# A transformer block on one core: transposes moved from TensorE to DMA, LN2 scale and shift in place, weight loads by rows

## The chip, the cores and the metric

The kernel runs on 1 core of one Trainium2 chip. The metric is device time in microseconds (us), the median of several runs. A profile is one execution; its span (first to last instruction) is about 1.8 us shorter than the device time. Engines: PE is TensorE (PEld its weight loads), DVE is VectorE, ACT is ScalarE, POOL is GpSimd, SP issues most DMAs. ACTq and SPq are the DMA-issuing instructions on ACT and SP. A packet is one record of a DMA engine; a transfer "lands" when its last packet has told its semaphore. Tile names in the profile's lines: soft holds the attention weights, pa is their product with v, xn a normalised token tile, hT the transposed LN2 rows, pacc the sums of wo or fc1.

## The reference

One diffusion-transformer block in bf16, B=2 batches of N=256 tokens, D=1152, two heads, F=4608:

```
mod = silu(c) @ w_mod                       # shift/scale/gate for attention and for the MLP
h   = layernorm(x) * (1 + scale_a) + shift_a
q, k, v = h @ wqkv
a   = softmax(q k^T / sqrt(576)) v @ wo
x   = x + gate_a * a
h2  = layernorm(x) * (1 + scale_m) + shift_m       # "LN2"
out = x + gate_m * (gelu(h2 @ w_fc1) @ w_fc2)
```

The 512 tokens are 4 token tiles of 128 (tiles 0, 1 are batch 0; tiles 2, 3 are batch 1). A matmul contracts over partitions, so two results have to be transposed: the attention weights before they meet v, and the normalised LN2 rows before they meet w_fc1.

## The kernel before

Weights stream from HBM through five buffers of 2.65 MB, all issued by SP in order: a buffer is loaded again as soon as its last reader is done. A section is loaded by rows (2304 contiguous bytes each) or by column panels (768 bytes each):

```python
    def load_section(name, s):                       # rows: 3 x 1152 elements
        for r in range(0, KD, 3):
            nc.sync.dma_start(w[:, r:r + 3, :], wmod_v[:, r:r + 3, s * D:(s + 1) * D])
    def load_panels(name, view, col0):               # panels: 9 x 384 elements
        for n in range(NPD):
            nc.sync.dma_start(w[:, :, n * PW:(n + 1) * PW], view[:, :, col0 + n * PW:col0 + (n + 1) * PW])
    ...
    w_v = load_panels("w_v", wqkv_v, 2 * D)
    w_o = load_panels("w_o", wo_v, 0)
    w_f1[0] = load_panels("w_f1_0", wfc1_v, 0)       # ... and w_f1[1]
    # ... after the v matmuls: w_f1[2], w_f1[3], w_gate_m
```

Attention weights are transposed on TensorE (16 matmuls against an identity) and evicted from PSUM. LN2 is transposed the same way, in pieces placed between the matmuls of wo (batch 0) and of the first fc1 outputs (batch 1); the eviction applies scale and shift:

```python
    def ln2_transpose(b, ks, eng):
        pt = aux_tile([P, len(ks), N], "pt", BF16)               # 2 PSUM buffers of this kind
        for i, k in enumerate(ks):
            for tl in range(TPB):
                nc.tensor.transpose(pt[:, i, tl * P:(tl + 1) * P], xn2[b * TPB + tl][:, k * P:(k + 1) * P], ident[:])
        for i, k in enumerate(ks):       # ACT or DVE: hT = pt * scale_m + shift_m
            ...
    order = [(t, i) for t in range(NT) for i in range(NPD)]      # 12 wo groups: token tile, column panel
    for o, (t, i) in enumerate(order):
        wo_group(t, i, ...)              # 9 matmuls; DVE: tmp = acc * gate; POOL: x1 = tmp + x
        if o: ln2_stats(*order[o - 1])   # DVE statistics; after a tile's last panel: sqrt (ACT), normalise
    ...
    MSPLIT = 10                          # first 10 fc1 outputs batch by batch, the others on 512 tokens
```

## Time and profile before

| | before |
|---|---|
| device time, median (3 runs) | 250.02 us (249.83 to 250.53) |
| span of the profile | 248.3 us |
| PE busy | 239.7 us |
| wo matmuls | 82.2 to 101.0 us |
| first fc1 matmul | 100.8 us |
| largest PE gap after the start | 0.99 us |

Lines of the page of the kernel before: the span, PE's busy time, and the chain of work that ended last, by engine.

```profile
span 248.3 us, 4032 instructions
PE 239.7 (97%) x1734; PEld 144.9 (58%) x1745; DVE 63.9 (26%) x172; ACT 69.1 (28%) x135; POOL 30.8 (12%) x46
PE 91%; DMA 3%; ACT 2%; DVE 1%; issue 1%; SPq 0%; ACTq 0%; DVEq 0%
```

PE bounds the kernel. The windows view of the kernel before shows the LN2 hand-over (columns: stretch, its length, busy us of each engine with the number of instructions, granted clock, DMA share of the 16 engines, GB/s):

```profile
100.00:108.00 8.00, 8.00 (x78) 6.98 (x76) 4.69 (x15) 5.15 (x8) 0.74 (x1) 1.00 1.10 332
108.00:116.00 8.00, 7.01 (x70) 6.19 (x68) 1.01 (x3) 5.06 (x10) 0.00 (x0) 1.00 0.80 297
```

PE is full from 100 to 108 us, has one gap of 1 us after it, and the DMA engines are full (share 1.10) beside it. The timeline of the same kernel (start, duration, engine, line, operation; in brackets the idle time before it and what ended it) names the gap:

```profile
106.04 1.28 ACT L674 ACT_TABLE_LOAD   x1
109.38 0.38 PE L582 MATMUL pt<-ident,xn 128*128 128x128 bf16 x4 [0.99 <-ACT hT L587]
```

PE waits for ACT to evict a transpose, and ACT is late because of a table load.

### The profile page before, as it was taken

How to read it: one execution, taken by the hardware profiler on the slowest of the kernel's cores; microseconds unless marked ns; L12 is line 12 of the kernel's file. 1: busy time of each engine (PE TensorE's matmuls, PEld its weight loads, DVE VectorE, ACT ScalarE, POOL GpSimd, SP SyncE). 2: the span in 40 equal slices, each digit the busy share in tenths (PEclk: the TensorE clock that was granted, in tenths of full speed). 3: DMA queues.
4: the chain of work that ended last, by engine and by line, in shares of the span. 5: the costliest groups of instructions: out<-in, count | busy, mean ns of one | idle time of the engine just before them, and what ended most of it. 6: DMA issues, size and time to landing. Idle time of an engine off the chain costs nothing.

```text
span 248.3 us, 4032 instructions
## 1 busy us (share of the span) xinstructions
PE 239.7 (97%) x1734; PEld 144.9 (58%) x1745; DVE 63.9 (26%) x172; ACT 69.1 (28%) x135; POOL 30.8 (12%) x46
## 2 busy tenths in 40 slices
PE   6799999999999999989999999999999999999994
PEld 2585444456657656878744444444565666656674
DVE  2852551335535588720001000000001100000001
ACT  7641341252424325593224222332000000000000
POOL 4000000021000255100003010000011122211111
PEclk9999999999999999999999999999999999999999
DMA  6999999999999999993194997490000000000000
GB/s 231 326 337 364 365 334 386 331 370 394 372 327 328 326 329 326 326 372 148 33 338 109 338 340 227 141 288 1 0 16 18 16 16 18 17 16 20 26 22 17
DMA packets 54285, 51.59 MB, mean 208 GB/s; under 512 B 1515, under 2 KB 47995, under 8 KB 54267
## 3 DMA queue, kind: packets, MB, share of 16 engines
q1 hardware_dynamic: 53664, 50.14, 64.0%
q0 software_dynamic: 576, 1.19, 1.4%
q8 instruction: 13, 0.21, 0.4%
q14 instruction: 5, 0.04, 0.1%
q10 hardware_dynamic: 27, 0.00, 0.0%
HBM read 50.14 MB, written 1.19 MB: 207 GB/s over the span
## 4 chain that ended last, share of the span: by engine, by line
PE 91%; DMA 3%; ACT 2%; DVE 1%; issue 1%; SPq 0%; ACTq 0%; DVEq 0%
PE pacc L704 28%; PE pacc L658 25%; PE pacc L488 7%; PE pacc L611 7%; PE pacc L436 7%; PE pk L265 5%; DMA w_scale_a<-in_w_mod_dram 3%; PE pk L298 2%; PE pa L544 2%; PE ps_s L464 2%; PE pn L381 1%; PE pg L414 1%; PE pm L233 1%; PE pt L243 1%; PE pt L582 1%
## 5 line engine op out<-in xcount | busy, mean ns | idle before, releaser
L704 PEld LDWEIGHTS <-gT 128*128 128x128 bf16 x468 | 44.4, 98 | 26.2
L710 DVE TENSOR_TENSOR tmp<-pacc,gate 128x384 f32<-128x384 f32 (+2 forms) x13 | 6.9, 527 | 103.8 <-PE pacc L704 103.8
L682 ACT ACTIVATE gT<-pacc 128x512 bf16<-128x512 f32 x26 | 15.5, 597 | 34.9 <-PE pacc L658 34.9
L712 POOL TENSOR_TENSOR o_sb<-tmp,x_1139 128x384 bf16<-128x384 f32 (+1 forms) x12 | 11.7, 972 | 88.9 <-DVE tmp L710 88.9
L488 PE MATMUL pacc<-w_v,hT 128*128 128x384 bf16 x108 | 19.2, 326 | 0.0
L704 PE MATMUL pacc<-w_f_2_1852,gT 128*128 128x384 bf16 (+2 forms) x117 | 18.9, 314 | 0.0
L658 PE MATMUL pacc<-hT,w_f_0_128 128*128 128x256 bf16 x162 | 18.8, 273 | 0.0
L704 PE MATMUL pacc<-w_f_1_1750,gT 128*128 128x384 bf16 x108 | 18.7, 326 | 0.0
L611 PE MATMUL pacc<-w_o,big_136 128*128 128x384 bf16 x108 | 18.5, 326 | 0.0
L704 PE MATMUL pacc<-w_f_3_1954,gT 128*128 128x384 bf16 (+2 forms) x135 | 18.4, 294 | 0.0
L704 PE MATMUL pacc<-w_f_0_1622,gT 128*128 128x384 bf16 x108 | 18.2, 326 | 0.0
L658 PE MATMUL pacc<-hT,w_f_1_132 128*128 128x512 bf16 (+1 forms) x88 | 17.9, 357 | 0.1
L436 PE MATMUL pacc<-hT,w_q 128*128 128x512 bf16 x79 | 17.7, 379 | 0.1
L658 PE MATMUL pacc<-hT,w_f_3_1047 128*128 128x512 bf16 x80 | 17.6, 379 | 0.1
L658 PE MATMUL pacc<-hT,w_f_2_1043 128*128 128x512 bf16 x79 | 17.5, 379 | 0.1
L658 PEld LDWEIGHTS <-w_f_0_128 128*128 128x128 bf16 x162 | 15.7, 98 | 1.8
L425 POOL DMA_DIRECT2D gates_dram<-nat x8 | 4.3, 543 | 79.6 <-DVE nat L422 79.6
L618 POOL TENSOR_TENSOR x_1139<-tmp,x_sb 128x384 f32<-128x384 f32 x11 | 10.0, 912 | 33.1 <-issue 27.0
L488 PEld LDWEIGHTS <-hT 128*128 128x128 bf16 x108 | 10.4, 98 | 6.3 <-issue 0.5
L611 PEld LDWEIGHTS <-big_136 128*128 128x128 bf16 x108 | 10.4, 98 | 6.2
L265 PE MATMUL pk<-big_136,w_k 128*128 128x256 bf16 (+2 forms) x88 | 13.3, 292 | 0.5 <-ACT big_136 L252 0.4
L658 PEld LDWEIGHTS <-w_f_1_132 128*128 128x128 bf16 x90 | 8.7, 98 | 8.5 <-issue 0.3
(119 smaller groups left out, 220.2 us busy)
## 6 DMA issues: line engine op xcount, KB each, us to landing
w_shift_a<-in_w_mod_dram SPq DMA_DIRECT2D x3, 864.0 KB, 11.1
w_q<-in_wqkv_dram SPq DMA_DIRECT2D x3, 864.0 KB, 12.3
w_gate_a<-in_w_mod_dram SPq DMA_DIRECT2D x3, 864.0 KB, 10.0
w_v<-in_wqkv_dram SPq DMA_DIRECT2D x3, 864.0 KB, 12.4
w_shift_m<-in_w_mod_dram SPq DMA_DIRECT2D x3, 864.0 KB, 10.2
w_scale_m<-in_w_mod_dram SPq DMA_DIRECT2D x3, 864.0 KB, 14.8
w_o<-in_wo_dram SPq DMA_DIRECT2D x3, 864.0 KB, 16.4
w_f_0_128<-in_w_fc_dram SPq DMA_DIRECT2D x3, 864.0 KB, 10.3
```

The costliest lines, as they stand in the source:

```text
L265: nc.tensor.matmul(pk[m][:, c0:c1], w_k[:, k, m * P:(m + 1) * P], hT0[:, k, c0:c1], start=(k == 0 and c0 == 0), stop=(k == KD - 1), skip_g ...
L298: nc.tensor.matmul(pk[m][:], w_k[:, k, m * P:(m + 1) * P], hT0[:, k, :], start=(k == 0), stop=(k == KD - 1),)
L436: nc.tensor.matmul(pacc[:], w_q[:, k, m * P:(m + 1) * P], hT[:, k, :], start=(k == 0), stop=(k == KD - 1),)
L464: nc.tensor.matmul(ps_s[:], qT[:, cc, q0:q0 + P], k_ap, start=(i == 0), stop=(i == len(chunks) - 1),)
L488: nc.tensor.matmul(pacc[:], hT[:, k, t * P:(t + 1) * P], w_v[:, k, pnl * PW:(pnl + 1) * PW], start=(k == 0), stop=(k == KD - 1),)
L611: nc.tensor.matmul(pacc[:], aT[:, k, t * P:(t + 1) * P], w_o[:, k, c0:c1], start=(k == 0), stop=(k == KD - 1),)
L618: (nc.gpsimd if pool_add else nc.vector).tensor_tensor(x1[:, t, c0:c1], tmp[:], x_sb[:, t, c0:c1], op=ALU.add)
L658: nc.tensor.matmul(dst, w_f1[m // KD][:, k, ml * P:(ml + 1) * P], hT[:, k, c0:c1], start=(k == 0), stop=(k == KD - 1),)
L682: nc.scalar.activation(gT[:, m, :], pacc[:], ACT.Gelu_apprx_tanh)
L704: nc.tensor.matmul(pacc[:], gT[:, kk, t * P:(t + 1) * P], w_f2[j][:, r, c0 - n * PW:c0 - n * PW + cw], start=(kk == 0), stop=(kk == KF - 1),)
L710: nc.vector.tensor_tensor(tmp[:], pacc[:], gate_m[:, b, c0:c0 + cw], op=ALU.mult)
L712: (nc.vector if last else nc.gpsimd).tensor_tensor(o_sb[:], tmp[:], x1[:, t, c0:c0 + cw], op=ALU.add)
```

## The change

The intent: take all transposes but LN1's off TensorE. Eight DMA transposes from SBUF to SBUF, issued by ACT, replace them; scale and shift are then applied in place on DVE. So that fc1 can begin while slices of hT still arrive, half of its first outputs step over the contraction (k outermost, six outputs at a time). w_v, w_o and fc1 are loaded by rows.

```diff
-    w_v = load_panels("w_v", wqkv_v, 2 * D)
+    w_v = load_rows("w_v", wqkv_v, 2 * D)          # w_o and w_f1[0..3] likewise
 ...
+    def attn_transpose(i):
+        pair = attn_all[:, TPB * i:TPB * (i + 1), :].rearrange("p i n -> p (i n)")
+        nc.scalar.dma_start_transpose(attnT_all[:, i, :].rearrange("p (c n) -> p c n", n=P), pair)
 ...                                                 # in the loop of the v groups:
+        if i >= 2 and i % 2 == 0 and i // 2 <= B * H:
+            attn_transpose(i // 2 - 1)
 ...                                                 # (16 nc.tensor.transpose and their evictions removed)
+    def ln2_modulate(b, k):
+        h = hT[:, k, b * N:(b + 1) * N]
+        nc.vector.tensor_scalar(
+            h, h, scale_m[:, k, b:b + 1], shift_m[:, k, b:b + 1], op0=ALU.mult, op1=ALU.add)
 ...                                                 # end of ln2_normalize (36 PE transposes removed):
+        nc.scalar.dma_start_transpose(hT[:, :, t * P:(t + 1) * P], xn2[:])
 ...
+    BETWEEN = {2: (0, 1), 3: (5,)}                   # scale/shift of batch 0 amid the statistics of tiles 2, 3
 ...
-    MSPLIT = 10
+    MSPLIT = 12
+    nc.scalar.activation(early_gelu[:], zeros[:, 0:1], ACT.Gelu_apprx_tanh)
+    # per batch: outputs 0..5 with k outermost, then 6..11 with k innermost;
+    # after batch 0: ln2_modulate(1, k) for all k
```

## The prediction

> **What bounds the kernel.** TensorE. The profile's first part has PE busy 239.7 of 248.3 us; the chain of waits is 91% PE. The windows by stage show granted clock 1.00 and from 84 us on one PE gap, 0.99 us, near 108.4: transposes wait for a PSUM buffer that ScalarE frees late (a gelu table load of 1.28 us at 106.0 delays it). DMA is saturated until about 112 us, but binds PE only in the first 9 us.
>
> **Removed from PE** (timeline and chain):
> - 16 transposes of the attention weights, 0.89 us.
> - 36 LN2 transposes; four take 0.22 us, so 1.98 us: half between the wo matmuls, half between the first fc1 matmuls.
> - The 0.99 us gap: nothing in fc1 waits for PSUM transposes any more, and an early gelu loads the table.
>
> Sum 3.86 us, all on the PE chain. The evictions that go too were off it.
>
> **Added or moved.** 18 in-place scale/shift operations on VectorE; the like one, hT<-big 128x256 bf16, takes 0.28 us. MSPLIT 12: two outputs as 2x256 columns instead of 512, neutral (0.109 against 0.219 us apiece in the chain). Eight DMA transposes on the ScalarE queue, 4 of 128 KB and 4 of 288 KB. No trace here times one. The Trainium skill ("DMA: Bandwidth & Descriptors", Latency and other measured facts) gives 261 GB/s with a non-contiguous middle dimension; from that I estimate 0.5 and 1.1 us of transfer, and beside saturated queues 2.5 to 5 us from issue to landing.
> Row-wise loads: a window with row sections (52 to 60 us) moves 389 GB/s, with panels (68 to 108 us) 327, so w_v, w_o and fc1 should each load about 1.2 us faster. That pays for the transposes' traffic and for needing all rows in the first group (last w_v panel landed near 53.4 us, needed by 53.8; w_o near 81.8, needed by 82.4). Stall under 0.3 us.
>
> **The critical place: LN2 into fc1.** wo should run from 81.4 to 99.0 us (12 groups of 1.465 us). Token tile 1's normalisation should end near 94.6, its transpose land at 98 to 99. VectorE waits for it in order, amid tile 2's statistics (near 97.4), and still owes two tmp, an add, three statistics, a normalise and seven modulations, about 6 us at 0.5 per large operation. fc1 eats one k slice per 0.65 us (6 matmuls of 0.109) and catches up with VectorE from k=2 to k=6. Estimated PE stall 0.5 to 2 us, about 1.1. Batch 1's transpose (issued near 104) has until 111: no stall. The attention transposes have over 6 us of slack.
>
> **Prediction.** 250.0 - 3.9 + 1.1 (hand-over) + 0.1 (loads), about 247.2 us; 8 in 10 between 245.7 and 249.4. Faster by over 2%: 0.05; within 2%: 0.91; slower by over 2%: 0.04.
>
> **What would show each step.** No PE transposes after 26 us; wo from 81.4 to 99.0; the waits list PE fc1 for VectorE hT, about 1 us, and VectorE hT for a DMA transpose, 0.5 to 2 us; PE waits for w_v or w_o under 0.3 us; PE busy near 237; DMA transposes landing in 2.5 to 5 us; GB/s near 380 between 68 and 100 us.
>
> **What would make it wrong.** A transpose that lands 8 us or later after issue (starved beside the weight stream): VectorE blocks, 250 us or more. Transposes that hold up the weight stream so that w_o lands late. Or a landing before 97: 246.1 us.

## The result

| | before | after |
|---|---|---|
| device time, median (4 runs each) | 250.11 us | 262.33 us (262.20 to 262.63) |
| ratio, 95% interval | | 1.0489 (1.0471 to 1.0507) |
| span of the profile | 248.3 us | 260.7 us |
| wo matmuls | 82.2 to 101.0 us | 82.3 to 100.1 us |
| first fc1 matmul | 100.8 us | 112.8 us |

A ratio here and below is the mean time of one kernel's runs over that of the other's of the same rounds, so not quite the ratio of the medians quoted. The outcome is slower by 4.9%, to which the prediction gave a chance of 0.04.

The page of the changed kernel, the lines that answer to those of before (and the granted clock in 40 slices of 6.5 us):

```profile
span 260.7 us, 3981 instructions
PE 239.1 (92%) x1700; PEld 144.7 (55%) x1711; DVE 66.9 (26%) x184; ACT 62.4 (24%) x124; POOL 28.0 (11%) x43
PEclk9999999999999998559999999999999999999999
PE 76%; DMA 15%; DVE 6%; ACT 1%; issue 1%; SPq 0%; DVEq 0%; ACTq 0%
```

15% of the chain is now DMA. Its windows over the same place:

```profile
92.00:100.00 8.00, 8.00 (x50) 4.63 (x48) 6.54 (x16) 1.21 (x2) 2.73 (x3) 1.00 1.09 359
100.00:108.00 8.00, 0.06 (x1) 0.00 (x0) 0.00 (x0) 0.29 (x1) 0.00 (x0) 0.66 1.08 389
108.00:116.00 8.00, 3.17 (x16) 2.28 (x17) 3.49 (x10) 1.35 (x1) 0.91 (x1) 0.50 0.70 251
```

PE, DVE and ACT stand still together from 100 to 112 us, while the DMA engines are full. The granted clock falls to half in the gap. The waits view (engine, line, what it waited for: us in all, times, longest) gives the sequence:

```profile
DVE hT L553 <- DMA hT<-xn: 16.5, 2, 13.4
PE pacc L631 <- DVE hT L553: 13.3, 2, 12.8
PE pa L541 <- DMA soft<-soft: 0.9, 1, 0.9
```

DVE waits 13.4 us for a DMA transpose, PE 12.8 us for DVE. The timeline of the changed kernel names the transpose, token tile 1's:

```profile
95.98 6.09 ACTq L573 DMA_TRANSPOSE hT<-xn  x1
112.44 0.60 DVE L553 TENSOR_SCALAR hT<-hT,scale_m,shift_m 128x256 bf16<-128x256 bf16 x2 [13.39 <-DMA hT<-xn]
112.83 5.90 PE L631 MATMUL pacc<-hT,w_f_0_128 128*128 128x256 bf16 x36 [12.78 <-DVE hT L553]
```

It was issued at 95.98 us and landed 16.4 us later. The same trace has a comparison within itself. Lines of the DMA view for 96 to 112 us, when tile 0's and tile 1's transposes move beside the weights (q1 is SP's queue, q10 ACT's: packets, MB, share of the 16 engines' time; then the issue in that window with its time to landing):

```profile
q1 hardware_dynamic: 2425, 5.36, 90.3%
q10 hardware_dynamic: 2363, 0.59, 18.6%
...
hT<-xn ACTq DMA_TRANSPOSE x1, 16.4
```

and for 116 to 117.6 us, when tile 2's moves alone; its issue, at 114.83 us, is the last line:

```profile
q10 hardware_dynamic: 1184, 0.30, 98.3%
...
hT<-xn ACTq DMA_TRANSPOSE x1, 3.2
```

Beside the stream, 2363 transpose packets of about 250 bytes (0.59 MB / 2363) went through in the time of 2425 weight packets of about 2210 bytes: one to one. It is so within the window too: from 98.4 to 103.6 us, 832 and 832. Two LN2 transposes took 16 us, 37 GB/s. Alone, one takes 1.6 us, 0.30 MB at about 185 GB/s, and lands 3.2 us after issue. The 5.36 MB that went in front are fc1 part 2's rest, part 3 and gate_m, weights that PE needed no earlier than 132 us (gate_m) and 139 us (fc1 part 2) in the kernel before.

Where the 12.4 us of span come from, each term read from the two traces:

| term | us |
|---|---|
| 52 PE transposes and the 0.99 us gap gone | -3.86 |
| PE waits for the last attention transpose | +0.88 |
| PE waits for tile 1's LN2 transpose | +12.78 |
| first 36 fc1 matmuls: 6.38 us (112.83 to 119.21) instead of 3.92 (36 x 0.109, the chain before has 8 in 0.87) | +2.46 |
| sum | +12.26 |

The last term holds both the half clock and DVE's remaining work; they are not separated here, but e2_hold below needs 6.17 us for the same matmuls at full clock, so the half clock's part seems small. The Trainium skill ("TensorE: Matmul & The Clock Gate", Part 1) says that an idle window of about 3.4 us halves the clock and about 3.4 us of work restores it. The trace agrees on the half clock and on the recovery, not on the idle time: the windows have clock 1.00 until 102.5 us, 0.50 from 102.6 to 116.2, and 1.00 after; PE had stopped at 100.1 (2.5 us before the drop, sooner than a whole window of 3.4) and begun again at 112.8 (3.4 us before the recovery).

### The profile page after: what moved, and what is told of

Its sections match the earlier page's. It is cut to its first block, busy times and chain, and to the rows that moved or that the text cites. A ratio compares the mean times of both kernels' runs of the same rounds, so it can differ in the third digit from the quotient of the medians.

```text
span 260.7 us, 3981 instructions
## 1 busy us (share of the span) xinstructions
PE 239.1 (92%) x1700; PEld 144.7 (55%) x1711; DVE 66.9 (26%) x184; ACT 62.4 (24%) x124; POOL 28.0 (11%) x43
## 4 chain that ended last, share of the span: by engine, by line
PE 76%; DMA 15%; DVE 6%; ACT 1%; issue 1%; SPq 0%; DVEq 0%; ACTq 0%
PE pacc L685 27%; PE pacc L631 25%; PE pacc L436 7%; DMA hT<-xn 6%; DMA w_f_1_132<-in_w_fc_dram 6%; PE pacc L488 6%; PE pk L265 4%; DMA w_scale_a<-in_w_mod_dram 3%; PE pk L298 2%; PE ps_s L464 2%; DVE tmp L587 1%; PE pn L381 1%; PE pg L414 1%; DVE hT L553 1%; PE pm L233 1%
## 5 line engine op out<-in xcount | busy, mean ns | idle before, releaser
L631 PE MATMUL pacc<-hT,w_f_0_128 128*128 128x256 bf16 x162 | 20.0, 287 | 13.3 <-DVE hT L553 13.3
L631 PEld LDWEIGHTS <-w_f_0_128 128*128 128x128 bf16 x162 | 16.6, 103 | 16.6 <-issue 13.9
L663 ACT ACTIVATE gT<-pacc 128x512 bf16<-128x512 f32 x24 | 14.3, 597 | 32.2 <-PE pacc L631 32.2
L631 PE MATMUL pacc<-hT,w_f_1_132 128*128 128x256 bf16 (+1 forms) x106 | 17.9, 325 | 0.1
L436 PE MATMUL pacc<-hT,w_q 128*128 128x512 bf16 x79 | 17.7, 379 | 0.1
L582 PE MATMUL pacc<-w_o,big_136 128*128 128x384 bf16 x108 | 17.7, 326 | 0.0
L582 PEld LDWEIGHTS <-big_136 128*128 128x128 bf16 x108 | 10.6, 98 | 6.9
L631 PEld LDWEIGHTS <-w_f_1_132 128*128 128x128 bf16 x108 | 10.5, 98 | 6.8 <-issue 0.3
L488 PEld LDWEIGHTS <-hT 128*128 128x128 bf16 x108 | 10.4, 98 | 6.3 <-issue 0.5
L631 PEld LDWEIGHTS <-w_f_2_1047 128*128 128x128 bf16 x81 | 7.9, 98 | 9.5
L631 PEld LDWEIGHTS <-w_f_3_1051 128*128 128x128 bf16 x81 | 7.9, 98 | 9.5
```

The costliest lines, as they stand in the source:

```text
L436: nc.tensor.matmul(pacc[:], w_q[:, k, m * P:(m + 1) * P], hT[:, k, :], start=(k == 0), stop=(k == KD - 1),)
L488: nc.tensor.matmul(pacc[:], hT[:, k, t * P:(t + 1) * P], w_v[:, k, pnl * PW:(pnl + 1) * PW], start=(k == 0), stop=(k == KD - 1),)
L582: nc.tensor.matmul(pacc[:], aT[:, k, t * P:(t + 1) * P], w_o[:, k, c0:c1], start=(k == 0), stop=(k == KD - 1),)
L631: nc.tensor.matmul(dst, w_f1[m // KD][:, k, ml * P:(ml + 1) * P], hT[:, k, c0:c1], start=start, stop=(k == KD - 1), **kw,)
L663: nc.scalar.activation(gT[:, m, :], pacc[:], ACT.Gelu_apprx_tanh)
```

## The experiments

Theory A: the weight stream starves the transposes. Each DMA engine lets one 256-byte transpose packet through per weight packet, so their pace is set by the stream, and PE waits for whatever the slack does not cover. Rivals: transposes are slow by themselves, or held by semaphores or by ACT's queue (B); the row-wise loads cost by themselves.

| label | time us | before, same rounds | ratio (95%) |
|---|---|---|---|
| e1_panels | 267.68 | 250.43 | 1.0681 (1.0629 to 1.0733) |
| e2_hold | 249.34 | 250.43 | 0.9959 (0.9943 to 0.9975) |
| e3_attn_dma | 248.94 | 250.43 | 0.9944 (0.9928 to 0.9961) |
| e4_rows | 250.22 | 250.43 | 0.9996 (0.9981 to 1.0010) |
| e5_panels_hold | 250.99 | 250.20 | 1.0031 (1.0018 to 1.0044) |
| e6_hold_pool | 247.39 | 250.20 | 0.9886 (0.9873 to 0.9898) |
| e7_panels_hold_pool | 248.83 | 250.20 | 0.9960 (0.9940 to 0.9981) |
| e8_hold_b0 | 262.16 | 250.20 | 1.0478 (1.0464 to 1.0492) |
| e9_f10_panels | 246.38 | 250.36 | 0.9843 (0.9828 to 0.9857) |
| e10_last_pair_pe | 246.77 | 250.36 | 0.9858 (0.9842 to 0.9875) |

All ten gave correct results.

### e2_hold: the late weights wait for the transposes

```diff
-    w_f1[2] = load_rows(...); w_f1[3] = load_rows(...); w_gate_m = load_rows(...)   # before LN2
+    def load_held(name, view, col0):
+        w = wide_tile(name)
+        for r in range(0, KD, 3):
+            nc.vector.memset(w[:, r:r + 1, 0:1], 0.0)     # DVE, so behind all it was given earlier
+            nc.sync.dma_start(w[:, r:r + 3, :], view[:, r:r + 3, col0:col0 + D])
+        return w
 ...
             for k in range(KD):
                 ln2_modulate(1, k)
+            # w_gate_m, w_f1[2], w_f1[3] = load_held(...)
```

> The changed kernel, row-wise loads kept, but the last three loads of the first wave (gate_m, fc1 parts 2 and 3, 8 MB) are held back until the LN2 transposes of batch 1 have landed, by a one-column memset of their tiles on VectorE behind the scale/shift. Theory A (the weight stream starves the transposes): LN2 transposes land in 3 to 4 us as the last two did after 112 us, the gap before fc1 falls from 12.8 to about 1 us, no clock drop, time 247.5 to 249.5 us. Theory B (transposes slow by themselves, or held by semaphores or by the ScalarE queue): tile 1 still lands 10 us or more after issue, time 258 or more.

It took 249.34 us, and all four LN2 transposes landed in 3.2 us. In the timeline of e2_hold tile 1's transpose, issued at nearly the same time, no longer holds PE, and fc1 begins at 99.8 us:

```profile
95.90 1.31 ACTq L577 DMA_TRANSPOSE hT<-xn  x1
99.20 0.60 DVE L557 TENSOR_SCALAR hT<-hT,scale_m,shift_m 128x256 bf16<-128x256 bf16 x2 [0.24 <-DMA hT<-xn]
99.81 1.47 PE L635 MATMUL pacc<-hT,w_f 128*128 128x256 bf16 x12
105.98 6.28 PE L635 MATMUL pacc<-hT,w_f 128*128 128x256 bf16 x56 [0.47 <-DVE hT L557]
```

Theory B falls: the instruction, its data, its queue and its place are the same; only the stream beside it is gone. What is left shows too: the first 36 matmuls take from 99.81 to 105.98, 6.17 us instead of 3.92, at full clock. The waits name DVE's hT.

### e1_panels: shorter weight packets

```diff
-    w_v = load_rows(...)        # w_o, w_f1[0..3] likewise
+    w_v = load_panels(...)
```

> The changed kernel with only the row-wise loads undone (w_v, w_o and the four fc1 loads by column panels, 768-byte packets, as before). Theory A (packet turns): on each DMA engine one 256-byte transpose packet goes through per weight packet, so its rate is set by the length of the weight packets: 93 ns + 18 ns beside rows, about 40 + 18 beside panels. Then the transpose of token tile 1 lands about 8 us after issue instead of 16.4, PE idles about 4 to 5 us before fc1 instead of 12.8, time 252 to 255 us. Theory B (transposes get a share by bytes, or are slow by themselves): landing stays at 15 to 17 us, time 261 to 263.

It took 267.68 us: outside both expectations, slower than the changed kernel. The pace bears out theory A in part only. The DMA view of e1_panels for 95.5 to 106 us, when the first two LN2 transposes move, and for two stretches within it, 96.4 to 102.8 and 103.2 to 105.8 us:

```profile
q1 hardware_dynamic: 2508, 1.90, 79.7%
q10 hardware_dynamic: 2355, 0.59, 38.6%
...
q1 hardware_dynamic: 1296, 0.98, 80.6%
q10 hardware_dynamic: 1124, 0.28, 37.2%
...
q1 hardware_dynamic: 886, 0.67, 76.7%
q10 hardware_dynamic: 884, 0.23, 38.4%
```

A weight packet is now 757 bytes on average, and the two transposes need 10.5 us (0.59 MB, 56 GB/s) instead of 16. The near-equal totals hide two paces. In the last stretch it is one to one, 886 and 884. Before it the counts swing (85 weight and 392 transpose packets from 97.2 to 98.0 us, 251 and 49 from 99.6 to 100.4), and less is moved: the weights go at 153 GB/s (0.98 MB in 6.4 us), against 258 in the last stretch. Why is open. So tile 1's landed 11.4 us after issue, not 8. And what the transposes win, the stream loses: weights moved at 181 GB/s in that window, against 335 in the changed kernel's (5.36 MB in 16 us). It then still ran when batch 1's transposes were issued at 109 and 114 us; in the changed kernel it had run out by then. The second of them landed 15.8 us after issue, and PE, which had begun 8.2 us late, stood still a second time. Two lines of its timeline, the first fc1 matmuls of batch 0 and of batch 1 (the first line puts its gap down to a weight load; the transpose behind DVE's hT was the later one to be ready, DVE having ended its wait for it at 106.80):

```profile
107.20 14.58 PE L631 MATMUL pacc<-hT,w_f 128*128 128x256 bf16 x108 [8.18 <-DMA w_f<-in_w_fc_dram]
130.20 2.10 PE L631 MATMUL pacc<-hT,w_f 128*128 128x256 bf16 x9 [8.43 <-DVE hT L553]
```

So the one-to-one turns are seen with two sizes of weight packets, with the smaller one in part of the time only. The time that I derived from them was wrong because they did not hold throughout, and because I counted only the first victim.

### e8_hold_b0: let the stream go one stage earlier

As e2_hold, but the three loads are let go after tile 1's transpose has landed (near 100 us) instead of after tile 3's.

```diff
+        if o == len(order) - 3:
+            # w_gate_m, w_f1[2], w_f1[3] = load_held(...)
```

> The held version with rows, but the three loads are let go as soon as batch 0's transposes have landed, so that only batch 1's transposes meet the stream. If a starved transpose costs whatever slack it doesn't have, batch 0 lands in 3 us, batch 1's second one 13 to 17 us after issue (near 121), and PE idles 8 to 11 us before batch 1 of fc1 instead of before batch 0: 257 to 261 us. Rival: only batch 0's transpose is critical, 249 to 251.

It took 262.16 us, 1.2 us above the range. Tiles 0 and 1 landed in 3.2 us, tiles 2 and 3 in 14.5 and 17.7 us. The waits of its PE:

```profile
PE pacc L639 <- DVE hT L557: 12.3, 4, 10.4
```

The gap has moved: 10.4 us before batch 1 of fc1. The rival (only batch 0's transpose matters) falls: a starved transpose of batch 1 costs PE as well, once the stream meets it.

### e3_attn_dma and e4_rows: one part alone on the kernel before

e3_attn_dma takes only the attention transposes from the change, e4_rows only the row-wise loads.

```diff
 # e3_attn_dma, on the kernel before
-    16 x nc.tensor.transpose(pTt..., attn_tiles...), 4 x evac(attnT, pTt[:])
+    4 x nc.scalar.dma_start_transpose(attnT_all[:, i, :]..., pair)      # in the v loop, as in the change
 # e4_rows, on the kernel before
-    w_v = load_panels(...)        # w_o, w_f1[0..3] likewise
+    w_v = load_rows(...)
```

> The kernel before with only the attention transposes moved to DMA (panels kept, LN2 on PE). Theory A: beside panels and row sections the four transposes land in about 6 to 8 us, before PE asks for them, so PE saves 0.89 us: 249.0 to 249.5. Theory B (as slow as in the changed kernel, 10 us, whatever the weight packets): the 0.9 us gap in the pa matmuls comes back, 249.8 to 250.4.

It took 248.94 us (span 247.3 against 248.3): 1.0 us of span, the 0.89 us of PE work and no new wait. They landed in 8.3 to 10.3 us (three of the four; no landing is recorded for the second), later than expected (part of the stream is loaded by rows in this kernel too), but the last one in 8.3; in the changed kernel that one took 10.5, and PE waited 0.88 us for it.

> The kernel before with only the row-wise loads. If these cost nothing by themselves: 249.8 to 250.4 us, GB/s near 385 instead of 327 between 68 and 100 us. Rival: needing all rows in the first group of v and of wo stalls PE, 251 or more, with PE waits for w_v or w_o.

It took 250.22 us. The windows of e4_rows:

```profile
68.00:100.00 32.00, 32.00 (x288) 21.16 (x286) 20.24 (x48) 12.21 (x22) 9.13 (x10) 1.00 1.03 383
```

PE has no gap, and the loads move at 383 GB/s where panels had 327. Rows are quicker, and needing all rows in the first group costs nothing; but PE does not wait for weights here, so nothing is won.

### e5, e6, e7: what is left, and two attempts on it

e2_hold still has two losses: the 0.88 us wait for the last attention transpose, and 2.25 us (6.17 - 3.92) in the first fc1 matmuls. e5_panels_hold takes panels for w_v, w_o and fc1 parts 0 and 1; e6_hold_pool moves scale/shift slices to GpSimd; e7 does both.

```diff
 # e5, on e2_hold
-    w_v = load_rows(...)          # w_o, w_f1[0], w_f1[1] likewise
+    w_v = load_panels(...)
 # e6, on e2_hold: slices of batch 0
-        if o == len(order) - 1:
-            ln2_modulate(0, 2); ln2_modulate(0, 3)           # DVE, then 4, 5, 6, 7, 8 on DVE
+        # after the statistics of tile 2: k = 2, 3 on nc.gpsimd; after the last wo group: k = 4, 5, 6 on nc.gpsimd
+    BETWEEN = {2: (0, 1), 3: (7, 8)}                          # DVE
```

> The held version (gate_m and fc1 parts 2 and 3 after the LN2 transposes), with w_v, w_o and fc1 parts 0 and 1 by column panels. If the 0.9 us gap in the pa matmuls comes from attention transposes alternating packet by packet with 2304-byte weight packets, it goes with 768-byte ones (as it did in e3_attn_dma) while the LN2 transposes still land in about 3 us: 248.2 to 248.8 us. If panels lengthen the stream of fc1 part 1 into the first LN2 transpose, that one lands later and the gain is lost: 249 or more.

It took 250.99 us, the second case: the attention gap went, but the stream of fc1 part 1, longer by panels, reached the LN2 transposes. Tiles 0 and 1 landed 8.9 and 5.6 us after issue, and PE waited 2.2 us.

> The held version with rows, and the scale/shift of batch 0, k=2 to 6, on GpSimd instead of VectorE (k=7, 8 earlier on VectorE). If what is left of the hand-over loss (36 matmuls of fc1 took 6.2 us instead of 3.9 in e2_hold) is VectorE's debt of other work between the slices, most of it goes: 247.3 to 248.2 us, fc1 waits for hT under 0.7 us. Rival: GpSimd is too slow at it or slows VectorE: 249 or more.

It took 247.39 us. In its timeline the first 24 fc1 matmuls run without a gap and the next wait 0.16 us:

```profile
99.93 2.78 PE L635 MATMUL pacc<-hT,w_f 128*128 128x256 bf16 x24
102.88 26.95 PE L635 MATMUL pacc<-hT,w_f 128*128 128x256 bf16 x218 [0.16 <-POOL hT L557]
```

The first 36 take 4.25 us instead of 6.17. So most of the 2.25 us of e2_hold (1.92) were DVE's debt: slices of hT queued behind gates, adds and statistics of the last wo groups.

> Both of the above together: 246.3 to 247.6 us if the two losses (attention gap, VectorE debt) are separate and add up; equal to the better of the two if they are not.

It took 248.83 us (two of its six runs 250.1 and 250.3): a miss. The two losses are separate, but panels on all four loads make a third one, as in e5 (PE waited 1.9 us before fc1).

### e9 and e10: the attention gap without lengthening the stream much

e9_f10_panels is e6_hold_pool with panels for fc1 part 0 alone. e10_last_pair_pe is e6_hold_pool with the last pair of attention tiles transposed by 4 PE matmuls.

```diff
 # e9, on e6
-    w_f1[0] = load_rows(...)
+    w_f1[0] = load_panels(...)
 # e10, on e6
-        if i >= 2 and i % 2 == 0 and i // 2 <= B * H:
+        if i >= 2 and i % 2 == 0 and i // 2 < B * H:
             attn_transpose(i // 2 - 1)
+    # after the v loop: 4 x nc.tensor.transpose of the last pair, evac into attnT_all[:, B * H - 1, :]
```

> e6_hold_pool with only fc1 part 0 by column panels: the load that streams while the third and fourth attention transposes move. If packet length sets their pace, the last one lands before 80 us, the 0.9 us gap in pa goes, and the stream ends about 1.2 us later, near enough to before the LN2 transposes to leave them at 3 to 4 us: 246.4 to 247.0 us. If the lengthened stream reaches the LN2 transposes, 247.4 or more.

> e6_hold_pool with the last of the four attention transposes back on TensorE (4 matmuls, 0.22 us), so that no pa matmul waits for a DMA transpose that was issued late: gap of 0.9 us gone, 0.22 us of PE work back, 246.6 to 247.0 us. Rival: the third transpose now makes the same gap, 247.3 or more.

e9 took 246.38 us: the last attention transpose landed 7.9 us after issue, at 78.6 us. The waits view of PE in e9_f10_panels from 40 us to the end has a single line:

```profile
PE pacc L635 <- POOL hT L557: 0.2, 1, 0.2
```

That packet length alone made the gap is not shown. In the changed kernel the two queues all but stop together from 78.5 to 79.8 us, while the last attention transpose moves; e2_hold and e6_hold_pool have such a stop at the same place, e4_rows and e10, where no transpose is under way there, have none, and in e9 the transpose had landed before. Without the stop (1.3 us) it would have landed near 79.9 us, an estimate from its landing at 81.2, and PE asked for it at 80.4. What causes the stop was not tested.

e10 took 246.77 us, also without the gap. Both beat both kernels; e9 is the best version found, 1.6% below the kernel before.

## Why the prediction was wrong

- **PE's savings: right.** The removed transposes and the gap were put at 3.86 us; the sum of the two traces closes with that figure to within 0.2 us, and e3_attn_dma, with the attention transposes alone (0.89 us of it), gained 1.0 us of span. wo ended at 100.1 instead of the predicted 99.0 us, by the attention wait.
- **The step that failed: "beside saturated queues 2.5 to 5 us from issue to landing".** Measured: 8.3 to 10.5 us for the attention transposes (three of four), 12.9 and 16.4 us for tiles 0 and 1 of LN2. I took a transfer time and added a few us for a busy queue, as if a transpose waited once. The runs show that beside the rows it pays at every packet: about 250 bytes per weight packet of 2210 bytes, 37 GB/s instead of about 185, and tile 1's also waits behind tile 0's. e2_hold gives 3.2 us, inside the predicted range, when the stream is held.
- **"its transpose land at 98 to 99"** followed from it: 112.4 us. DVE blocked there as described, but for 13.4 us instead of 0.5 to 2. The prediction named this case ("starved beside the weight stream") and gave slower a chance of 0.04, although it had read that the DMA engines were full until 112 us.
- **"That pays for the transposes' traffic"** compared bytes per second. Bytes were not the matter: rows gave the stream 383 instead of 327 GB/s (e4_rows), and made each turn of a transpose packet longer. e1_panels shows that the reverse choice does not repair it.
- **"The attention transposes have over 6 us of slack"**: true of the slack, but the last landed 10.5 us after issue, and PE waited 0.88 us. The stall put down to loads (0.1 us) did not occur as such; no PE wait for w_v or w_o is in the trace.
- **"Batch 1's transpose ... no stall"**: right in the changed kernel, but by luck: the delay had emptied the stream. e8_hold_b0 shows the stall (10.4 us).
- **Hand-over by DVE, about 1.1 us**: the mechanism was right and the size was off. e2_hold measures 2.25 us at full clock, and e6_hold_pool removes 1.92 of it by taking slices off DVE.
- **The clock** was not thought of: a gap of 12.8 us halves it for 3.4 us of work after the gap.

Left open: beside the stream, the first packet of a transpose moves about 4 us after its issue (tile 0's was issued at 91.99 us and ACT's queue has no packet in the DMA view of 92.0 to 95.9 us), alone after about 1.2 us. What holds it for those 4 us was not tested, nor what makes both queues slow or stop for a time (e1_panels, and the changed kernel from 78.5 us). The packet records do not name the DMA engine, so the turns are not seen engine by engine. But their times fit single turns: from 98.5 to 103.5 us of the changed kernel a weight packet starts 2 to 4 ns before a transpose packet ends 1436 times, against 477 and 495 times in the 2 ns on either side; for a transpose packet that starts there is no such peak (308 times).

## What to carry to other kernels

Work moved from a full engine to DMA is not free where the DMA engines are full: beside the rows here, a transfer of small packets got one turn per packet of the bulk stream. So estimate its time as its packets per DMA engine times the time of one packet of each kind (here 1184 / 16 packets times 0.11 us, the 93 + 18 ns of the expectation of e1_panels: 8 us for each LN2 transpose, where two took 16), take it as a lower bound (e1_panels needed more), and compare it with the slack of its first reader. Prefetches that are not due soon are the thing to move: holding back 8 MB that were due more than 15 us later turned a loss of 4.9% into a gain of 0.4%, and clearing the smaller waits behind it made that 1.6%. When a transfer is late, look for the next victim before you shorten the first one's wait (e1, e5, e7 and e8 all moved the stall instead of removing it).

## What the Trainium skill lacked or had wrong

- "DMA: Bandwidth & Descriptors", Queues, rings and completion order, says that a DMA engine turns between queues packet by packet, with typically about 9 to 17 descriptors in a packet. For a DMA transpose beside a weight load the records show turns of one for one: 2363 transfers of about 250 bytes for 2425 of about 2210 bytes, and with panels 884 for 886 in one stretch (103.2 to 105.8 us of e1_panels), not throughout. The page does not say what this does to a transpose: 16.4 us to landing instead of 3.2.
- "DMA: Bandwidth & Descriptors", Rules for kernel authors, says that a transpose next to ordinary DMAs needs nothing. That holds for the results, which were correct in every run; for the time it does not (changed kernel 262.33 us, e2_hold 249.34).
- The same page, Latency and other measured facts, gives 261 GB/s for a DMA transpose with a non-contiguous middle dimension, and "Advanced Engine Details and Errata", X-Bar Transpose (TRN2), says transposes are as fast as regular DMAs. Alone on the engines, one of 0.30 MB moved in 1.6 us, about 185 GB/s, where row-wise weight loads moved 383.
- No page has a time on this chip for issuing a DMA transpose from ACT ("DMA: Bandwidth & Descriptors" has only cycle counts, in a passage on trn3), or says that it grows beside other traffic: 1.3 us for the 288 KB ones when alone (e2_hold), up to 6.1 us beside the stream, during which ACT does nothing else.
